# Spatial mixing of a gated MLP: the Strassen level on one chunk pair extended to both pairs, on shared combinations, with partial sums kept in PSUM

## The chip, the cores and the metric

One Trainium2 core runs the kernel; the other cores are idle. The metric is device time in microseconds, the median of 3 runs. All data are fp32 in HBM. TensorE multiplies in a reduced fp32 form, so each product of the kernel is made of three matmuls: every operand is split into a high half (written by ScalarE) and a low half (the difference, by VectorE, which the profile calls DVE), and high x high, high x low and low x high are added up in PSUM.

## The reference

```
xn = layernorm(x)                                    # 2048 x 512
# branch A: 32 heads of 16, each position attends to 8 positions, 2 apart, behind it
q, k, v = xn @ wqkv;   s = softmax(q . k[pos - 2w] / 4) . v[pos - 2w] @ wo
# branch B: gated MLP with mixing over positions
z  = gelu(xn @ w_in)                                 # 2048 x 1792
z1, z2 = z[:, :896], layernorm(z[:, 896:])
g  = w_sp @ z2 + b_sp[:, None]                       # w_sp 2048 x 2048: the spatial mixing
b  = (z1 * g) @ w_out
out = x + s * silu(b)
```

## The kernel before

The work on TensorE runs in six stages, in this order. (1) The projection to q, k and v (`product`, lines 366 to 375). (2) z1 (lines 571 to 591): seven column blocks f of 128, times four chunks c of 512 positions, transposed, stored to HBM as `z1_d` (the profile says z_d). (3) z2 (lines 593 to 666): sixteen row tiles j of 128 positions, 896 columns in two halves of 512 and 384. (4) The spatial mixing (lines 717 to 896), the stage that the change rewrites. (5) The projection with w_out (tile b, `proj` at line 905, loop at 916), sixteen row tiles of 21 matmuls. (6) The projection with wo (tile s, loop at 947), sixteen row tiles of 12 matmuls, then gate, residual and store.

**The mixing.** Its result g has seven column blocks f of 128 and four chunks c of 512 output positions. The sum runs over the sixteen z2 tiles. Chunks 2 and 3 are computed densely (line 717): for each of sixteen weight blocks and each of seven f, three matmuls of 512 columns into PSUM tile g. When a chunk is done, VectorE adds the bias for those tiles that weren't seeded with it (line 739), multiplies by z1 (line 741), and the result is parked in HBM (`g_d`); `late` fetches it again and splits it.

Chunks 0 and 1 go by one Strassen level: the weights form a 2 x 2 block matrix (chunk 0 or 1; the upper eight position tiles or the lower eight), and z2 another (upper or lower tiles; first three column blocks or last three). The middle block f = 3 is computed apart (`odd_upper`, `odd_lower`). `block_sums` (line 557) prepares the four sums of weight blocks that Strassen needs, for one position tile at a call: two loads of 512 KB, four VectorE additions of 512 columns, two stores of 512 KB to `sums_d`. `combine` (line 635) makes the four combinations T of z2 blocks in place and stores them to `t_d`; `operand` (line 749) loads two position tiles of one T and splits them into the space of the last three z2 blocks, where the original is no longer needed. `block_product` (line 760) runs one of the seven products, in four steps of two position tiles: 72 matmuls, or 96 where the middle block goes along; after each step it calls what `steps` lists. In the order p1, p2, q6, q7, q5, q3, q4 the products use the plain weights or the sums; PSUM results are copied to SBUF by ScalarE (lines 844, 882) and joined by VectorE subtractions (`minus`, line 804).

**z2 statistics.** `z2_stats` (line 614) has VectorE do two BATCH_NORM_STATS of 448 columns and one aggregation for each of sixteen tiles, then GpSimd makes the scale and shift. `z2_normal` has ScalarE normalise 896 columns in place (line 627) and then splits them.

**Attention** (line 478) is VectorE work almost alone: eight passes `sub`, each over four heads and all positions, in four steps j0 of four position tiles. A step multiplies (line 503), reduces (506), after the softmax multiplies again (530), adds in a tree (536 to 538), transposes (545) and stores to `o_d`. All of it has the lowest priority (`LOW`, lines 476 and 480).

**What sets the order.** Engines work in the order in which instructions stand on their queues. Some instructions are pinned in program order (`pin`); the rest is ordered when the kernel is compiled, by a list scheduler that simulates the time line and, among the instructions that are ready, takes the highest priority. Attention is thus placed where VectorE has nothing else that is ready.

**Buffers.** PSUM has eight banks, taken in turn by `mm`. Weights go through four raw buffers (`RAW`) and eight split pairs. Eight tiles of 1024 columns (`WIDE`, `t4`) serve z1, z2, sums, T operands and the last stage. `load_o` (line 675) fetches attention output for one group of four row tiles, one 128-row operand k of four at a time, each from two `sub` passes; k = 3 has the last one. The last stage takes the groups in the order 0, 2, 3, 1 (line 942), that is steps j0 = 0, 8, 12, 4 of each pass.

## Time and profile before

| | |
|---|---|
| median of 3 runs | 708.52 us (708.4 to 708.57) |
| profiled execution: time | 708.39 us |
| profiled execution: span, first to last instruction | 706.6 us |
| granted TensorE clock, mean | 0.999 |
| busy: TensorE / VectorE / ScalarE / GpSimd | 700.7 / 619.2 / 260.9 / 41.8 us |
| HBM read / written | 100.40 / 50.94 MB |

The stages on TensorE, from the time line of PE:

| stage | from | to |
|---|---|---|
| z2 | 227 (about 219 with its first tiles) | 294.8 |
| spatial mixing, dense chunks 2 and 3 | 294.8 | 447.2 |
| spatial mixing, chunks 0 and 1 by Strassen | 447.2 | 583.0 |
| projection with w_out | 583.0 | 659.15 |
| projection with wo | 659.15 | 703 |

A duration in a row of PE is that of one matmul from start to end, about 390 ns at 512 columns; they overlap, and their pace is the distance of two starts. A VectorE row of 0.69 us can likewise be followed after 0.60. A row of the time line gives start, duration, engine, line, operation, output <- inputs, shapes, and in brackets the idle time before it with what ended it. A row of the windows view gives the window, its length, then busy time and instruction count of PE, PEld, DVE, ACT and POOL, the granted clock, the busy share of the DMA engines and GB/s.

### The profile page before, as it was taken

To read this page: it belongs to the slowest core of one execution; us is meant where nothing else is said; L and a number is where in the kernel's file an instruction comes from. 1 tells how busy PE (TensorE), PEld (TensorE's weight loads), DVE (VectorE), ACT (ScalarE), POOL (GpSimd) and SP (SyncE) were. 2 spreads that over 40 slices of the span, in tenths; PEclk is the share of its full clock that TensorE was granted. 3 is DMA by queue.
4 is the path that set the end of the run, shared out by engine and by line. 5 is a ranking of instruction groups with operands and counts; after the bars stand their busy time and mean duration, and the time that the engine had idled before them with its cause. 6 is when DMAs were issued, how large, how long until landed. Compare 5 with 4: busy or idle time off the path is not lost.

```text
span 706.6 us, 8920 instructions
## 1 busy us (share of the span) xinstructions
PE 700.7 (99%) x3152; PEld 585.4 (83%) x3152; DVE 619.2 (88%) x770; ACT 260.9 (37%) x403; POOL 41.8 (6%) x81
## 2 busy tenths in 40 slices
PE   8999999999999999999999999999999999999997
PEld 7888888888888988888888888888888888888886
DVE  6774599989998899989999999999999999799665
ACT  4343332343224466751112211354545542131531
POOL 3100000000000443320000000000000000000000
PEclk9999999999999999999999999999999999999999
DMA  8767775585785131579956742877857781353996
GB/s 271 255 189 228 240 242 178 161 287 207 258 275 220 33 135 69 190 255 323 328 183 219 288 135 60 307 239 260 276 200 269 246 260 59 125 165 101 303 327 235
DMA packets 96652, 151.93 MB, mean 215 GB/s; under 512 B 8672, under 2 KB 50912, under 8 KB 96608
## 3 DMA queue, kind: packets, MB, share of 16 engines
q1 hardware_dynamic: 57968, 108.77, 47.1%
q10 hardware_dynamic: 38640, 42.60, 17.3%
q8 instruction: 24, 0.39, 0.2%
q14 instruction: 20, 0.16, 0.1%
HBM read 100.40 MB, written 50.94 MB: 214 GB/s over the span
## 4 chain that ended last, share of the span: by engine, by line
PE 98%; DMA 1%; DVE 0%; SPq 0%; issue 0%
PE g L695 22%; PE q L695 12%; PE p L695 6%; PE qkv L371 6%; PE qkv L373 6%; PE qkv L372 6%; PE z L608 4%; PE z L607 4%; PE z L606 4%; PE z L580 4%; PE b L911 4%; PE z L578 4%; PE b L910 4%; PE b L912 4%; PE z L579 4%; PE s L911 2%
## 5 line engine op out<-in xcount | busy, mean ns | idle before, releaser
L503 DVE TENSOR_TENSOR pr<-k,q 128x2048 f32<-128x2048 f32 x32 | 73.2, 2286 | 1.9 <-DMA q<-qkv_d 1.5
L530 DVE TENSOR_TENSOR pv<-v,lg 128x2048 f32<-128x2048 f32 x32 | 73.3, 2291 | 0.9
L506 DVE TENSOR_REDUCE lg<-pr 128x128 f32<-128x2048 f32 x32 | 73.0, 2281 | 0.4
L391 ACT ACTIVATE stage<-qkv 128x512 f32<-128x512 f32 x36 | 21.4, 596 | 49.2 <-PE qkv L373 49.1
L536 DVE TENSOR_TENSOR pv<-pv 128x1024 f32<-128x1024 f32 x32 | 39.1, 1221 | 0.5
L608 PE MATMUL z<-w_0h,BIG 128*128 128x512 f32 x64 | 25.0, 391 | 0.0
L607 PE MATMUL z<-w_0l,BIG 128*128 128x512 f32 x64 | 25.0, 391 | 0.0
L606 PE MATMUL z<-w_0h,BIG 128*128 128x512 f32 x64 | 24.9, 389 | 0.0
L921 ACT ACTIVATE bt<-b 128x512 f32<-128x512 f32 x16 | 9.4, 597 | 41.5 <-PE b L912 41.5
L627 ACT ACTIVATE zt<-zt,nmz,mvz 128x896 f32<-128x896 f32 x16 | 17.9, 1134 | 17.6 <-POOL nmz L623 17.3
L267 DVE TENSOR_TENSOR xT<-xT,mr 128x512 f32<-128x512 f32 x20 | 13.8, 688 | 11.2 <-DMA mr<-mv_d 6.6
L537 DVE TENSOR_TENSOR pv<-pv 128x512 f32<-128x512 f32 x32 | 22.0, 687 | 0.6
L608 PE MATMUL z<-w_1h,BIG 128*128 128x384 f32 x64 | 21.5, 336 | 0.0
L606 PE MATMUL z<-w_1h,BIG 128*128 128x384 f32 x64 | 21.5, 335 | 0.0
L607 PE MATMUL z<-w_1l,BIG 128*128 128x384 f32 x64 | 21.4, 335 | 0.0
L587 ACT ACTIVATE z1t<-z 128x512 f32<-128x512 f32 x21 | 12.5, 594 | 21.8 <-PE z L580 21.8
L965 DVE TENSOR_TENSOR sg<-s,sg 128x512 f32<-128x512 f32 (+1 forms) x17 | 11.2, 657 | 10.6 <-PE s L912 9.7
L618 DVE BATCH_NORM_STATS2 zst<-zt 128x6 f32<-128x448 f32 x32 | 19.1, 610 | 1.5 <-ACT zt L609 1.5
L620 POOL TENSOR_TENSOR nmz<-mvz,mone 128x1 f32<-128x1 f32 x16 | 5.0, 315 | 234.8 <-DVE mvz L619 234.7
L184 DVE TENSOR_TENSOR BIG<-zt,BIG 128x896 fp32r<-128x896 f32 x16 | 17.1, 1079 | 1.1 <-ACT BIG L183 1.1
L609 ACT ACTIVATE zt<-z 128x512 f32<-128x512 f32 (+1 forms) x24 | 12.8, 535 | 13.4 <-PE z L608 12.1
L373 PE MATMUL qkv<-wqkv_0h,BIG 128*128 128x512 f32 x43 | 16.7, 389 | 0.0
(543 smaller groups left out, 2164.1 us busy)
## 6 DMA issues: line engine op xcount, KB each, us to landing
qkv_d<-stage ACTq DMA_DIRECT2D x24, 512.0 KB
k<-qkv_d SPq DMA_DIRECT2D x8, 960.0 KB
v<-qkv_d SPq DMA_DIRECT2D x8, 960.0 KB
z_d<-z1t ACTq DMA_DIRECT2D x14, 512.0 KB
t_d<-zt ACTq DMA_DIRECT2D x16, 384.0 KB
zl<-z_d SPq DMA_DIRECT2D x12, 512.0 KB
tr<-t_d SPq DMA_DIRECT2D x16, 384.0 KB
x<-in_x SPq DMA_DIRECT2D x16, 256.0 KB
```

The costliest lines, as they stand in the source:

```text
L371: nc.tensor.matmul(pq, xh[:, k], wh, start=k == 0, stop=False)
L372: nc.tensor.matmul(pq, xh[:, k], wl, start=False, stop=False)
L373: nc.tensor.matmul(pq, xl[:, k], wh, start=False, stop=k == KB - 1)
L503: nc.vector.tensor_tensor(pr, taps(kw, j0), qb.unsqueeze(1).to_broadcast([P, W, NJ * CS]), op=ALU.mult)
L506: nc.vector.tensor_reduce(lg[:, :, j0 * HS : (j0 + NJ) * HS], pr.rearrange("p w (i d) -> p w i d", d=DH), axis=AX.X, op=ALU.add,)
L530: nc.vector.tensor_tensor(pr.rearrange("p w (i d) -> p w i d", d=DH), taps(vw, j0).rearrange("p w (i d) -> p w i d", d=DH), lg[:, :, j0 * ...
L536: nc.vector.tensor_tensor(pr[:, 0:4], pr[:, 0:4], pr[:, 4:8], op=ALU.add)
L606: nc.tensor.matmul(pz, xh[:, k], wh, start=k == 0, stop=False)
L607: nc.tensor.matmul(pz, xh[:, k], wl, start=False, stop=False)
L608: nc.tensor.matmul(pz, xl[:, k], wh, start=False, stop=k == KB - 1)
L695: nc.tensor.matmul(pg, z[a], w[b], start=start and i == 0, stop=stop and i == 2, skip_group_check=seeded)
L911: nc.tensor.matmul(pp[:, cols], hi, wl, start=False, stop=False)
```

## The change

Chunks 2 and 3 are no longer dense. Both chunk pairs go by the same Strassen level, and each of the seven products is run for the pair (2, 3) and right behind it for the pair (0, 1), so that a T operand is loaded once for two products. The order is p1, p2, q6, q5, q3, q7, q4, each for c = 2 and then for c = 0. Pair 2 has PSUM banks 4 to 7, pair 0 has 0 to 3. The signs of the combinations are chosen so that p1 + p2 + ... can go on adding in the same PSUM banks: after p1 ScalarE copies the banks to SBUF (`snapshot`), p2 adds on, after p2 the first three column blocks are gated from PSUM, the banks are seeded with the copy (`seeded`), q6 adds on, is copied, q5 adds on, is copied, and q3 adds on; q7 and q4 start from the bias. The bias is always a seed. The parked `g_d` goes; the copies after q6 are parked in `y_d` and loaded again for q4's results.

`block_sums` makes the sums of both pairs, sixteen calls for eight: seven in the z1 stage (`SUMS_Z1`), three in z2 (`SUMS_Z2`, in raw buffers), six in the steps of p1 and p2. `z2_stats` leaves VectorE: the Gelu's accumulator gives the sum, a ScalarE Square over 896 columns the variance, and GpSimd has five small operations for four. `z2_normal` splits only the first four column blocks of the upper tiles. In the last two upper and lower tiles the 384-column PSUM tile is filled with zeros by VectorE first and accumulated on. The place of the gated tiles in SBUF (`slots`) and the rows of `b_sp` are rearranged.

The diff, cut to its core:

```diff
-    def block_sums(i):
-        top, low = t4(f"sa_{i}"), t4(f"sb_{i}")
...
+    def block_sums(n, own=False):
+        c, i = 2 - n // HT * 2, n % HT
...
-        if f % 2:
-            block_sums(f // 2)
+        if f in SUMS_Z1:
+            block_sums(next(summed))
...
+        keep = h == 1 and j % HT > HT - 3
+        if keep:
+            nc.vector.memset(pz, 0.0)
...
-        nc.scalar.activation(zt[:, HALF[h]], pz, AF.Gelu_apprx_tanh, scale=late_rstd(j))
+        nc.scalar.activation(
+            zt[:, HALF[h]], pz, AF.Gelu_apprx_tanh, scale=late_rstd(j), accum_out=sumz[:, j, h : h + 1]
+        )
...
-        for h in range(2):
-            nc.vector.bn_stats(st[:, h], zt[:, h * FQ : (h + 1) * FQ])
-        nc.vector.bn_aggr(mv, st)
-        nc.gpsimd.tensor_tensor(nm, mv[:, 0:1], mone, op=ALU.mult)
-        nc.gpsimd.tensor_scalar(mv[:, 1:2], mv[:, 1:2], EPS, None, op0=ALU.add)
+        nc.gpsimd.tensor_tensor(mv[:, 0:1], sz[:, 0:1], sz[:, 1:2], op=ALU.add)
+        nc.gpsimd.tensor_scalar(mv[:, 0:1], mv[:, 0:1], -1.0 / FH, None, op0=ALU.mult)
+        nc.scalar.activation(
+            z2_at(j)[0], blocks(zt, FB), AF.Square, bias=mv[:, 0:1], accum_out=mv[:, 1:2]
+        )
+        nc.gpsimd.tensor_scalar(
+            mv[:, 1:2], mv[:, 1:2], 1.0 / FH, EPS, op0=ALU.mult, op1=ALU.add
+        )
...
-        split(zh, zl, blocks(zt, FB))
+        n = FB if j >= HT else ODD + 1
+        split(zh[:, :n], zl[:, :n], blocks(zt, FB)[:, :n])
...
-    for c in (2, 3):
-        for n, js in enumerate(order):
...
-                three(banks[key], z2_block(js, f), w, n == 0 and key not in seeds, n == NT - 1, key in seeds)
...
+    for c, b in ((2, bb[:, 1]), (0, bb[:, 0])):
+        seeded(c, "p", [b] * 3)
+        odd_[c] = seed(BANKS[c] + 3, f"oa_{c}", b)
+        if c == 2:
+            product_("p1", 2, upper, first_weights, odd_upper, ([], [sums_step], [], [sums_step]))
+    first = three_halves("s")
+    snapshot((*first[2], o1[2]), (*acc[2], odd_[2]))
+    product_("p1", 0, upper, w_sp[0, :HT], odd_upper, ([], [sums_step], [], [sums_step]))
+    snapshot((*first[0], o1[0]), (*acc[0], odd_[0]))
+    product_("p2", 2, lower, w_sp[2, HT:], odd_lower, ([T2[0]], [T2[1], sums_step], [T2[2]], [T2[3], sums_step]))
...
+    product_("p2", 0, lower, w_sp[0, HT:], odd_lower, ([g[0]], [g[1]], [], []))
+    seeded(2, "y", first[2])
+    g = first_result(0)
+    product_("q6", 2, turned, ws(2, 2), steps=([g[0]], [g[1]], [later(seeded, 0, "y", first[0])], []))
...
+    product_(
+        "q6", 0, turned, ws(0, 2),
+        steps=([later(snapshot, yv[2], acc[2]), later(store_y, 0)], [T1[0]], [T1[1]], [T1[2]]),
+    )
...
+    product_("q5", 0, turned, ws(0, 1), steps=([later(snapshot, ev[2], acc[2])], [], [], []))
...
+    product_(
+        "q3", 2, lower_right, ws(2, 4),
+        steps=([T3[0], later(snapshot, ev[0], acc[0])], [T3[1]], [T3[2]], [T3[3]]),
+    )
...
+    product_(
+        "q4", 2, turned, w_sp[3, HT:], odd_lower, steps=([T4[3], g[0]], [g[1]], [load_y], [])
+    )
...
```

More of the change, by code (lines that the diff above doesn't have):

```diff
@@ L46 @@
 WARM = 8
+SUMS_Z1 = range(7)
+SUMS_Z2 = (1, 2, 3)
 RAW = 4
@@ L658 @@
                 if i == HT - 1 and h == 0:
-                    spatial[2, HT] = spatial_block(2, HT)
+                    for js in range(2):
+                        spatial[2, js] = spatial_block(2, js)
+        if i in SUMS_Z2:
+            block_sums(next(summed), own=True)
         if 0 < i <= HT:
@@ L826, in lower_first @@
-    def lower_first(f0):
-        zl = z1_pair(1, f0, 2)
-        for f in (f0, f0 + 1):
-            v = vv[f] if f < ODD else o1
-            if f < ODD:
-                minus(v, v, banks["q", f])
-            else:
-                minus(v, banks["o", 1], v)
-            gated(1, f, v, zl[:, f - f0])
-    T1, T2, T3, T4 = [[later(operand, i, h, s0) for s0 in range(0, HT, 2)] for i, h in ((0, 0), (1, 1), (1, 0), (0, 1))]
-    block_product("p1", "p", upper, lambda s: w_sp[0, s], (0, odd_upper), start=False)
```

334 lines of the change are left out of this document (169 added, 165 removed), and 4 rows, old and new, of the table slots.

## The prediction

> **What bounds the kernel now.** I read the page's engine totals first, then its forty slices, then the chain of work that ended last.
>
> ```profile
> span 706.6 us, 8920 instructions
> PE 700.7 (99%) x3152; PEld 585.4 (83%) x3152; DVE 619.2 (88%) x770; ACT 260.9 (37%) x403; POOL 41.8 (6%) x81
> PE   8999999999999999999999999999999999999997
> DVE  6774599989998899989999999999999999799665
> ...
> 294.80 152.36 PE g L695 x672
> 447.16 43.52 PE p L695 x192
> ```
>
> TensorE is busy in every slice, and the chain runs through it for 98% of the span. The last two rows give its pace: 152.36/672 and 43.52/192 are both 0.2267 us per 512-column matmul, with no pause in 196 us. So a matmul less is 0.2267 us less, as long as nothing else comes late. The second row to read is DVE: from the sixth slice to the thirty-fourth it is nearly as full as TensorE. The windows view gives the stretch from just before the first attention work (80.4) to the last (658.65), then the z2 stage:
>
> ```profile
> 80.40:658.65 578.25, 578.25 (x2595) 484.29 (x2594) 545.42 (x626) 215.27 (x332) 31.70 (x64) 1.00 0.62 207
> 227.00:295.00 68.00, 68.00 (x339) 61.12 (x338) 65.32 (x94) 39.43 (x57) 25.09 (x51) 1.00 0.25 86
> ```
>
> DVE (third busy number) works 545.42 of 578.25 us. Attention is emitted at the lowest priority, so it fills whatever time the other DVE work leaves, and its end tells how much DVE time there was. The DVE, SP and PE timelines show how close that end is to the output projection (tile s), which needs it:
>
> ```profile
> 640.23 0.45 DVE L545 STREAM_TRANSPOSE tt<-pv 128x256 f32<-128x256 f32 x1
> 648.31 0.69 DVE L184 TENSOR_TENSOR BIG<-ol,BIG 128x512 fp32r<-128x512 f32 x1
> 651.36 0.45 DVE L545 STREAM_TRANSPOSE tt<-pv 128x256 f32<-128x256 f32 x1
> 658.20 0.45 DVE L545 STREAM_TRANSPOSE tt<-pv 128x256 f32<-128x256 f32 x1
> 663.22 0.69 DVE L184 TENSOR_TENSOR o_3l<-ol,o_3h 128x512 fp32r<-128x512 f32 x1 [0.45 <-ACT o_3h L183]
> 676.95 0.69 DVE L184 TENSOR_TENSOR o_3l<-ol,o_3h 128x512 fp32r<-128x512 f32 x1 [3.23 <-ACT o_3h L183]
> ...
> 659.15 0.39 PE L910 MATMUL s<-BIG 128*128 128x512 f32 x1
> 702.71 0.28 PE L912 MATMUL s<-BIG,o_3l 128*128 128x256 f32 x1
> ```
>
> The projection runs in four row groups of 48 matmuls, 10.9 us each. The fourth operand of a group (k=3) holds the last attention block (sub 7) and is first used 9 matmuls, 2.0 us, into it. Group one needs it at 659.15+2.0 = 661.2 and has it at 649.0: 12.2 us to spare. Group two needs it at 672.1, has it at 663.9: 8.2 us. Group three needs it at 682.9, has it at 677.6: 5.3 us. That is all the slack, and it is less than what the change takes off TensorE. So two engines bound this kernel.
>
> **TensorE's part.** Before, the spatial mixing is 2 dense chunks x 16 blocks x 7 columns x 3 = 672 matmuls, and seven products of 96 or 72 = 600; 1272. After, it is 600 for each of two pairs; 1200. 72 x 0.2267 = 16.3 us. No other matmul is added or removed. By this alone the span is 690.3 and the time, with the 1.8 us that the profiled run has outside its span (708.39 against 706.6; the median of the runs, 708.52, is 0.13 higher), 692.1. The projection would start at 642.8.
>
> **DVE's part, counted instruction by instruction.** The groups by line:
>
> ```profile
> L618 DVE BATCH_NORM_STATS2 zst<-zt 128x6 f32<-128x448 f32 x32 | 19.1, 610 | 1.5 <-ACT zt L609 1.5
> L619 DVE BATCH_NORM_AGGREGATE mvz<-zst 128x2 f32<-128x12 f32 x16 | 2.9, 194 | 0.0
> L184 DVE TENSOR_TENSOR BIG<-zt,BIG 128x896 fp32r<-128x896 f32 x16 | 17.1, 1079 | 1.1 <-ACT BIG L183 1.1
> L739 DVE TENSOR_TENSOR gt<-g,bb 128x512 f32<-128x512 f32 x8 | 5.4, 682 | 0.0
> L804 DVE TENSOR_TENSOR ya<-q,ya 128x512 f32<-128x512 f32 x4 | 2.7, 686 | 0.0
> L567 DVE TENSOR_TENSOR sb<-sa,sb 128x512 f32<-128x512 f32 x16 | 10.9, 684 | 1.8 <-issue 1.4 <-DMA sb<-in_w_sp 0.5
> L184 DVE TENSOR_TENSOR q_7l<-q_7r,q_7h 128x512 fp32r<-128x512 f32 x5 | 3.4, 686 | 0.0
> L378 DVE MEMSET mask<- 128x128 f32 x1 | 0.2, 165 | 0.0
> ```
>
> Removed: the z2 statistics, 19.1 + 2.9 = 22.0; half of eight z2 splits (512 columns instead of 896), 8 x (1.079 - 0.684) = 3.2; the eight bias additions, 5.4; two subtractions (14 remain of 16), 1.4. Together 32.0. Added: the weight sums of the second pair, 32 x 0.684 = 21.9; 24 more low-half splits of weights (112 blocks for 32 + 56), 24 x 0.686 = 16.5; a bias addition of 1024 columns for one of 512, about 0.5; four zero fills of 384 columns, 0.165 for 128 columns, so 0.2 to 0.7 each, taken 0.4, 1.6 in all. Together 40.5. The gates, the splits of the gated tiles, the T operands and the four combinations keep their number. Net +8.5 us on DVE. Some instructions start 0.60 after the one before instead of 0.69, on both sides of the account alike, so I keep 8.5, with 7 to 10 as bounds.
>
> **What that does to the end.** The last attention block ends 8.5 later, at 667, if DVE's idle time of 32.8 us stays. Group one's k=3 is then ready at 649.0 + 8.5 = 657.5, and TensorE, there at 642.8 + 2.0 = 644.9 (rounded), waits 12.6 us. The time is 692.1 + 12.6 = 704.7; the same from the other side, 708.4 + 8.5 - 12.2. For groups two and three the same step with their own slack gives 708.4 + 8.5 - 8.2 = 708.7 and 708.4 + 8.5 - 5.3 = 711.6. I take group one's. Its k=3 followed its attention block by 8.3 us (640.7 to 649.0), the others' by 12 and 19, and the SP queue shows why the last did:
>
> ```profile
> 662.02 1.90 SPq L548 DMA_DIRECT2D o_d<-tt  x4
> 669.66 0.53 SPq L971 DMA_DIRECT2D out<-sg  x1
> 671.34 3.13 SPq L678 DMA_DIRECT2D ol<-o_d  x3
> ```
>
> Group three's loads stand behind an output store that waits for the projection itself, so they move with the projection, not with attention. With 8.3 us, group two (block ended 651.8) has its operand at 651.8 + 8.5 + 8.3 = 668.6, where a projection shifted to 655.4 asks for it at 668.3: no further wait to speak of. If the idle of 32.8 shrinks by 5, 699.7.
>
> **What is hidden.** ScalarE takes over the z2 variance:
>
> ```profile
> L627 ACT ACTIVATE zt<-zt,nmz,mvz 128x896 f32<-128x896 f32 x16 | 17.9, 1134 | 17.6 <-POOL nmz L623 17.3 <-DVE mvz L619 0.3
> L183 ACT ACTIVATE wsp_13h<-wsp_13r 128x512 fp32r<-128x512 f32 x2 | 1.2, 618 | 0.0
> L844 ACT ACTIVATE ya<-p 128x512 f32<-128x512 f32 x2 | 1.2, 600 | 1.4 <-PE p L695 1.4
> ```
>
> Sixteen squarings by the 1.134 row are 18.1 us; in the z2 stage ScalarE goes from 39.4 to about 57 of 68 us. In program order, the normalisation stands behind the squaring and the next Gelu behind that, but two steps' PSUM tiles (four of eight banks each) lie between them and TensorE: nothing on the path. Later ScalarE gets 24 high halves x 0.618 = 14.8, some 13 more snapshots and 8 more seeds x 0.600 = 12.6. Each seed or snapshot falls while TensorE works on the other pair's product, 72 x 0.2267 = 16.3 us; the cover is a whole product, and if it is gone a product pays 3 x 0.6 = 1.8 us. The first products need only the upper z2 tiles, the last of them 72 matmuls after the stage begins. DMA carries more as well:
>
> ```profile
> DMA packets 96652, 151.93 MB, mean 215 GB/s; under 512 B 8672, under 2 KB 50912, under 8 KB 96608
> 660.00:680.00 20.00, 20.00 (x89) 16.54 (x89) 11.03 (x15) 6.35 (x8) 0.00 (x0) 1.00 1.02 316
> ```
>
> The second pair's sums (8.4 MB read, 8.4 written, 8.4 read back) and 6 MB more direct weights replace 8.4 MB of dense weights and 7 of parked gates, and y is parked for 3: about 19 MB on 151.93, so 171 MB in some 695 us, 246 GB/s. The fullest window moved 316 (its last two numbers: the share of the engines, GB/s), so on average the fetches, four tiles ahead, hide it.
>
> **The rivals.** *TensorE alone decides* (692 to 697). For it: the chain is 98% PE, and DVE still has 32.8 us of idle; if the new, denser mix fills about 12 of it, attention ends by 655 and nothing waits. Against it: much of the idle stands in front of splits that wait for ScalarE's halves, and ScalarE gets more of them. *The late groups decide* (711.6, slower). The place is group three's k=3, with 5.3 us of slack; the price is 8.5, so 3.2 us over the time before. It decides if the way from block to operand stays at 19 us. For it: DMA around there is full, a share of 1.02 in the window from 660 to 680. Against it: these transfers are the projection's own. *A pause slows TensorE afterwards* (706 to 708.6). A pause of 12 us on TensorE occurs nowhere here, but the opening shows a cold start:
>
> ```profile
> 1.35 3.78 PE L276 MATMUL warm<-ident 128*128 128x128 f32 x16 [1.35 <-POOL ident masks.py:199]
> 6.16 0.61 PE L276 MATMUL warm<-ident 128*128 128x128 f32 x4
> ```
>
> The same matmul takes 3.78/16 = 0.236 us first and 0.61/4 = 0.153 later, so a restart costs about 16 x 0.083 = 1.3 us, and up to three groups can restart: 704.7 + 1.3 to 3.9. The Trainium skill (TensorE: Matmul & The Clock Gate, Part 1) says that after an idle window of about 3.4 us the array runs at half clock until it has been busy for such a window; by that rule a pause of 12 us costs an estimated 1.7 us more, 706.4. The opening rows agree with the direction, though the granted clock reads 1.00 there; a pause in mid-kernel no row shows. *New waits inside the products* (705 to over 712): a zero fill waits for its PSUM bank and holds what DVE has behind it; a sum's two stores wait on ScalarE's queue for four additions, 4 x 0.684 = 2.7 us, with weight halves, snapshots and seeds behind them. For it: these queues are in order and the chain has no pause now. Against it: 16.3 us of the other pair's product lie over each. If all fourteen products paid the 1.8 us, it would be 25 us, so the place matters more than the price.
>
> **How the numbers follow.** Forecast, attention's end with group one's slack, 698 to 708.7: 0.40. TensorE alone: 0.20. Late groups: 0.22. Cold restarts on top: 0.10. Waits inside the products: 0.08. A measurement here can tell about 0.2%, so "same" is 707.0 to 709.8. Faster: nearly all of the forecast's chance (0.36), 0.20, a third of the cold case (0.03), 0.02; 0.61. Same: 0.04 + 0.05 + 0.03 from these and 0.01 from the products; 0.13. Slower: the rest, 0.26. The range runs from TensorE's floor, 692.0, to the late groups', 711.6; the forecast's own is 698 to 708.7.
>
> **What would show it.** Line 695's successor has 1200 matmuls at 0.2267. DVE is busy about 627 us. The last transpose of attention ends near 667, and the first pause of TensorE over 2 us stands in the projection, released by an o operand, around 645 to 657. If TensorE has no pause there, the forecast is wrong on the fast side; if attention ends at 667 and the pauses are in groups two and three, it is the late groups; if TensorE pauses before the projection, the step that failed is that the products' waits are hidden.

## The result and the profile after

The changed kernel takes 720.22 us (median of 4 runs, 718.18 to 720.89) against 708.46 us before (4 runs, 708.14 to 708.57): a ratio of 1.0162, interval 1.0141 to 1.0183. The forecast was 704.7 with a range of 692.0 to 711.6, so it is wrong, on the other side. The profiled execution took 718.18 us, 716.4 of it span, which is 9.8 us more than the span before. Of the runs reported below, one of e4 (1835 us) and one of e12 (3979 us) were disturbed and are left out; both were the profiled ones, so that e4 was run again, and of e12's profile only the order of the instructions is used.

The page of the changed kernel: totals, TensorE's slices and clock, and the chain by engine.

```profile
span 716.4 us, 9058 instructions
PE 689.0 (96%) x3080; PEld 573.3 (80%) x3080; DVE 624.7 (87%) x771; ACT 300.3 (42%) x512; POOL 51.1 (7%) x97
PE   8999999999999999599999999999999999999973
PEclk9999999999999999899999999999999999999997
...
PE 81%; DMA 6%; DVE 4%; ACT 3%; issue 2%; SPq 1%; POOL 1%; ACTq 1%; DVEq 0%
```

The counts are near the predicted ones: 72 matmuls fewer, DVE at 624.7 us (627 predicted), 170.8 MB of DMA (171 predicted). What is new is the 5 in TensorE's seventeenth slice, at 286.6 to 304.5 us, with a dip in the clock under it, and two lean slices at the end. TensorE's share of the chain fell from 98% to 81%. TensorE's waits over the whole span, with total, number and longest:

```profile
PE p L734 <- ACT wsp_0h L188: 6.6, 1, 6.6
PE s L966 <- ACT o_3h L188: 3.6, 1, 3.6
PE s L966 <- DVE sg L1021: 1.4, 1, 1.4
...
PE z L633 <- ACT zt L637: 1.1, 1, 1.1
```

The TensorE and DVE timelines give the stage borders and the last attention transpose:

```profile
302.94 1.65 PE L734 MATMUL p<-wsp_0h,BIG 128*128 128x512 f32 x3 [6.61 <-ACT wsp_0h L188]
...
681.56 0.45 DVE L550 STREAM_TRANSPOSE tt<-pv 128x256 f32<-128x256 f32 x1
...
653.35 0.39 PE L966 MATMUL s<-BIG 128*128 128x512 f32 x1
...
704.12 0.28 PE L968 MATMUL s<-BIG,o_3l 128*128 128x256 f32 x1
```

The mixing begins at 302.94 (before: 294.63), the next stage at 577.19 (582.99), the projection at 653.35 (659.15), and the last matmul ends at 704.40 (702.99). So the 9.8 us are:

| part | us |
|---|---|
| 72 matmuls fewer | -16.3 |
| z2 stage ends later and TensorE pauses before the products | +8.3 |
| within the products (half clock after the pause, a gap of 0.4) | +2.2 |
| projection: 51.05 us instead of 43.84 (pauses of 3.6 and 1.4, slow matmuls after the first) | +7.2 |
| from the last matmul to the end: 12.0 us instead of 3.6 | +8.4 |

There are two places of loss: the z2 stage at 300 us, 10.5 us, and the projection with its tail, 15.6 us.

**The first place.** Around the pause the windows show TensorE idle (0.39 busy of 7) and VectorE and ScalarE full; the clock (third number from the end) then takes 3 us to come back:

```profile
80.40:682.00 601.60, 592.13 (x2645) 494.16 (x2643) 560.58 (x639) 260.00 (x449) 41.42 (x80) 0.99 0.70 236
296.00:303.00 7.00, 0.39 (x3) 0.07 (x2) 6.88 (x8) 6.97 (x16) 2.46 (x8) 0.71 0.36 123
303.00:306.00 3.00, 3.00 (x8) 2.21 (x9) 3.00 (x6) 3.00 (x7) 2.10 (x3) 0.53 0.71 248
306.00:310.00 4.00, 4.00 (x19) 3.29 (x18) 4.00 (x5) 4.00 (x10) 1.80 (x4) 1.00 1.01 400
```

ScalarE's timeline says what it does while TensorE waits for the first weight half (wsp_0h):

```profile
263.44 1.05 ACT L648 ACTIVATE BIG<-zt,mvz 128x896 fp32r<-128x896 f32 x1 [1.75 <-POOL mvz L647]
264.39 0.19 ACT L648 ACTIVATION_READ_ACCUMULATOR BIG<-zt,mvz 128x1 f32 x1
...
266.69 1.14 ACT L659 ACTIVATE zt<-zt,nmz,mvz 128x896 f32<-128x896 f32 x1 [1.66 <-POOL nmz L655]
...
302.27 0.62 ACT L188 ACTIVATE wsp_0h<-wsp_0r 128x512 fp32r<-128x512 f32 x1
...
307.98 0.48 ACT L637 ACTIVATE zt<-z 128x384 f32<-128x384 f32 x1
```

The Squaring (L648) waits 1.75 us for a mean that GpSimd forms, the normalisation (L659) 1.66 us for GpSimd's next steps. Every instruction with a sum beside its output is followed by a second one of 0.19 us. TensorE's last z2 matmul started at 296.00, and its Gelu runs at 307.98: ScalarE is 12 us behind, and the weight half sits in its queue. The change had also moved that half: the kernel before split the first weight block ahead of z2, at 201.7 (`early_pair`), and the changed kernel asks for it only near the end of z2. The four seeds of the first product were written by 299.7, so by an estimate about 3.2 of the 6.6 us (302.9 - 299.7) would go if the early split had stayed; no run restores it. It matters only when ScalarE is late: e1 and e17 below do without it and have no pause. Over 219 to 330 us ScalarE's waits add up to:

```profile
ACT zt L659 <- POOL nmz L655: 11.0, 7, 2.2
ACT BIG L648 <- POOL mvz L647: 10.7, 6, 2.9
```

**The second place.** The last attention block ends at 682.0; before it was 658.65. In the window from 80.4 to its end, VectorE works 560.58 of 601.60 us and idles 41.0 (before: 545.42, idle 32.8). So the end moved by 23.4 us = 15.2 more work in the window + 8.2 more idle. Only 5.5 of the 15.2 is work that the change added (624.7 - 619.2 over the whole kernel). The other 9.7 is VectorE work of later stages, which was done behind attention's end before and is now ahead of it. When the last block is there, SyncE's queue brings what is left late:

```profile
692.16 0.36 SPq L1027 DMA_DIRECT2D out<-sg  x1
692.63 1.28 SPq L717 DMA_DIRECT2D ol<-o_d  x1
...
696.68 0.33 SPq L988 DMA_DIRECT2D sg<-b_d  x1
```

The last operand load and the four pairs of loads for the last outputs (696.68 to 700.11) stand behind output stores, and are issued when TensorE is nearly through. In the chain that ended last, the load issued at 699.61 takes 8.7 us to land, at 708.4, and the last gates follow it. That is the tail.

### The profile page after: what moved, and what is told of

The parts are those of the page before. It is cut to its first block, busy times and chain, and to the rows that moved or that the text cites. A ratio compares the mean times of both kernels' runs of the same rounds, so it can differ in the third digit from the quotient of the medians.

```text
span 716.4 us, 9058 instructions
## 1 busy us (share of the span) xinstructions
PE 689.0 (96%) x3080; PEld 573.3 (80%) x3080; DVE 624.7 (87%) x771; ACT 300.3 (42%) x512; POOL 51.1 (7%) x97
## 4 chain that ended last, share of the span: by engine, by line
PE 81%; DMA 6%; DVE 4%; ACT 3%; issue 2%; SPq 1%; POOL 1%; ACTq 1%; DVEq 0%
PE y L734 14%; PE q L734 9%; PE p L734 8%; PE z L633 7%; PE qkv L378 4%; PE qkv L377 4%; PE qkv L376 4%; PE z L601 4%; PE b L968 4%; PE b L967 4%; PE z L600 4%; PE z L602 4%; PE b L966 4%; PE ob L734 3%; PE oa L734 3%
## 5 line engine op out<-in xcount | busy, mean ns | idle before, releaser
L508 DVE TENSOR_TENSOR pr<-k,q 128x2048 f32<-128x2048 f32 x32 | 73.1, 2285 | 2.7 <-DMA q<-qkv_d 2.4
L511 DVE TENSOR_REDUCE lg<-pr 128x128 f32<-128x2048 f32 x32 | 73.0, 2280 | 0.4
L633 PE MATMUL z<-w_0h,BIG 128*128 128x512 f32 x128 | 41.3, 392 | 1.1 <-ACT zt L637 1.1
L541 DVE TENSOR_TENSOR pv<-pv 128x1024 f32<-128x1024 f32 x32 | 39.0, 1218 | 0.3
L633 PE MATMUL z<-w_1h,BIG 128*128 128x384 f32 x128 | 34.0, 336 | 0.0
L633 PEld LDWEIGHTS z<-w_0h,BIG 128*128 128x128 f32 x128 | 24.0, 188 | 6.6 <-ACT zt L637 1.8
L582 DVE TENSOR_TENSOR sa<-sa,sa 128x512 f32<-128x512 f32 x39 | 26.5, 681 | 2.0 <-DMA sa<-in_w_sp 1.6
L646 POOL TENSOR_TENSOR mvz<-sumz 128x1 f32<-128x1 f32 x16 | 9.7, 605 | 204.7 <-ACT zt L637 204.7
L633 PEld LDWEIGHTS z<-w_1h,BIG 128*128 128x128 f32 x128 | 23.3, 188 | 0.3
L609 ACT ACTIVATE z1t<-z 128x512 f32<-128x512 f32 x21 | 12.4, 592 | 25.0 <-PE z L602 18.5
L659 ACT ACTIVATE zt<-zt,nmz,mvz 128x896 f32<-128x896 f32 x16 | 18.1, 1134 | 11.2 <-POOL nmz L655 11.0
L189 DVE TENSOR_TENSOR BIG<-zt,BIG 128x512 fp32r<-128x512 f32 (+1 forms) x16 | 14.2, 888 | 9.3 <-ACT BIG L188 9.1
L648 ACT ACTIVATE BIG<-zt,mvz 128x896 fp32r<-128x896 f32 x16 | 16.6, 1039 | 12.4 <-POOL mvz L647 10.7
L188 ACT ACTIVATE BIG<-zl 128x512 fp32r<-128x512 f32 x28 | 17.3, 621 | 10.0 <-DVE zl L807 8.5
L188 ACT ACTIVATE BIG<-tr 128x768 fp32r<-128x768 f32 x16 | 13.4, 843 | 17.8 <-PE q L734 9.1
```

What stands on the lines that cost most here:

```text
L188: first_ = pin(nc.scalar.activation(hi, src, AF.Copy))
L508: nc.vector.tensor_tensor(pr, taps(kw, j0), qb.unsqueeze(1).to_broadcast([P, W, NJ * CS]), op=ALU.mult)
L511: nc.vector.tensor_reduce(lg[:, :, j0 * HS : (j0 + NJ) * HS], pr.rearrange("p w (i d) -> p w i d", d=DH), axis=AX.X, op=ALU.add,)
L541: nc.vector.tensor_tensor(pr[:, 0:4], pr[:, 0:4], pr[:, 4:8], op=ALU.add)
L633: nc.tensor.matmul(pz, a[:, k], b, start=k + i == 0 and not keep, stop=k == KB - 1 and i == 2, skip_group_check=keep,)
```

## The experiments

Two theories stood at the start. A: VectorE's amount of work, through attention's end, sets the time. B: the pause after z2 does. Each kernel was timed beside the kernel before on the same chip, whose median was 708.2 to 708.5. Ratios are to that.

**Statistics back on VectorE (e1).** The changed kernel, with the z2 statistics as before (lines joined and cut):

```
-        nc.scalar.activation(z2_at(j)[0], ..., AF.Square, bias=mv[:, 0:1], accum_out=mv[:, 1:2])
+            nc.vector.bn_stats(st[:, h], zt[:, h * FQ : (h + 1) * FQ])
+        nc.vector.bn_aggr(mv, st)
```

> The changed kernel with the z2 statistics on VectorE again, as before the change; all else stays. Theory A (attention's end on VectorE sets the end, and the pause in front of the products only moves TensorE's idle time): the pause of 6.6 us goes, VectorE gets 22.0 us more work and loses some 12 us of idle time in the z2 stage, so attention ends near 692 instead of 682 and the time is about 730. Theory B (the z2 stage, now bound by ScalarE, is the main loss): z2 ends at 294.8 and the products follow without a pause, and the time is about 710.

Measured: 725.61 us (724.41 to 729.04), ratio 1.0252 [1.0223, 1.0280]. The mixing begins at 294.7, so the pause after z2 is gone. But VectorE is busy 642.4 us, the last transpose comes at 692.5, and the products and the projection wait:

```profile
PE y L734 <- DVE pv L544: 9.6, 1, 9.6
PE s L966 <- ACT o_3h L190: 5.6, 1, 5.6
```

So the pause is not all: taking it away by loading VectorE costs more. A stands, B alone falls.

**The weight sums on GpSimd (e2), and both edits together (e3).**

```
-            nc.vector.tensor_tensor(parts[out_], parts[a], parts[b], op=ALU.add)
+            nc.gpsimd.tensor_tensor(parts[out_], parts[a], parts[b], op=ALU.add)
```

> The changed kernel with all 64 additions of the weight sums on GpSimd instead of VectorE. VectorE loses 64 x 0.684 = 43.8 us of work, GpSimd gets about 64 x 1.3 = 83 us. Theory A: attention ends near 639, no wait is left in the last projection and its tail is 3.6 us as before; the pause in the z2 stage stays, so 692.1 + 10.5 = 702.6. Theory B: the same place loses less, since the z2 stage sets the end: 715 or more. Rival: GpSimd's additions delay the small GpSimd steps of the z2 statistics or VectorE itself, and nothing is won: 720 or more.

> Both edits at once: z2 statistics on VectorE, weight sums on GpSimd. VectorE's work is 21.8 us less than in the changed kernel and its waits for ScalarE in the z2 stage go, so attention ends near 649 and TensorE does not wait anywhere: 692 to 696. If a limit other than VectorE's work and the z2 stage holds the changed kernel back (DMA, or the order of the last loads), it stays above 702.

Measured: e2 737.30 (737.08 to 737.84), 1.0410 [1.0393, 1.0427]; e3 732.99 (730.20 to 733.48), 1.0340 [1.0320, 1.0360]. VectorE lost 64 additions of 0.684 us, 43.8 us, and yet its busy time rose from 624.7 to 636.8. The groups of e2, attention's operations and the additions (busy, mean ns):

```profile
L508 DVE TENSOR_TENSOR pr<-k,q 128x2048 f32<-128x2048 f32 x32 | 78.0, 2438 | 1.6 <-DMA q<-qkv_d 1.2
...
L511 DVE TENSOR_REDUCE lg<-pr 128x128 f32<-128x2048 f32 x32 | 73.0, 2280 | 0.3
L541 DVE TENSOR_TENSOR pv<-pv 128x1024 f32<-128x1024 f32 x32 | 45.4, 1418 | 0.4
L542 DVE TENSOR_TENSOR pv<-pv 128x512 f32<-128x512 f32 x32 | 27.1, 847 | 0.6
```

```profile
L582 POOL TENSOR_TENSOR sa<-sa,sa 128x512 f32<-128x512 f32 x39 | 68.0, 1745 | 190.5 <-DMA z_d<-z1t 111.1 <-DMA sa<-in_w_sp 33.5 <-ACT w_1h L188 14.4
```

In the changed kernel the same VectorE rows are 2285, 2280, 1218 and 684 ns: the two-input operations of these rows got 7 to 24% slower, the one-input reduction not at all. Splits that fell beside GpSimd's additions suffered most (the three of p_7l took 1768 ns in the mean, 682 in the changed kernel). The Trainium skill (SBUF — State Buffer, Who interferes with whom) says that a VectorE instruction with two SBUF inputs contends with a GpSimd instruction that reads SBUF, and that a reduction does not. The rows agree. GpSimd cannot take all of this work here; a part of it was not tried.

**Half of attention left out (e5).** The changed kernel, with four of the eight attention passes computed and stored twice:

```
-    for sub in range(NSUB):
+    for sub in range(0, NSUB, 2):
```

> The changed kernel with four attention passes of eight computed; each result is stored for two passes, so the attention output of every second pass is that of its neighbour. VectorE loses about 190 us of work. What is left is what the mixing costs without attention's end behind it: under both theories the pause in the z2 stage stays and the last projection has no wait, 702 to 704. If it comes to 692, the pause was itself attention's doing; if it stays above 710, the late end is not attention's.

Measured: 714.14 us (711.51 to 717.36), 1.0081 [1.0055, 1.0107]. By its number this is above 710, the expectation's case that the late end is not attention's; the trace says otherwise. VectorE is busy 466.6 us, the projection takes 43.8 us without a wait and 4.4 us follow it: the second loss is attention's. The time stays high because the first loss stays and is larger: the mixing begins at 310.7 instead of 302.9.

```profile
310.73 1.65 PE L735 MATMUL p<-wsp_0h,BIG 128*128 128x512 f32 x3 [9.56 <-ACT wsp_0h L188]
```

So the two losses have different causes, and the pause is not VectorE's amount of work.

**The statistics alone (e4), in the kernel before.** Only z2_stats is exchanged, and the two Gelus give their sums.

> The kernel before with only the z2 statistics moved to ScalarE, as the change does it; mixing, sums and order stay as before. VectorE has 22.0 us less. Theory C (the z2 stage itself is bound by ScalarE and the way over GpSimd, whatever follows): a pause of some 8 to 10 us between z2 and the mixing, 716 to 719, with attention ending earlier. Rival (the pause comes only from the changed kernel's seeds, sums and weight splits in that stage): no pause, 708.4.

> The kernel before with the z2 statistics on ScalarE once more, for its profile; the first time gave 724.0, some 16 us over the kernel before. Theory C: TensorE pauses 10 to 16 us in z2 and between z2 and the mixing, waiting for ScalarE, and nowhere else, while attention ends 15 us or more ahead of 658.65. Rival: the loss sits at the end, behind attention, and the z2 stage has no pause.

Measured: 724.03 and, run again, 723.84 us (723.28 to 724.40), 1.0216 [1.0195, 1.0236]. No Strassen level is added, VectorE has 18 us less to do (601.3), attention ends at 653.6, five us early, and the kernel is 15.5 us slower. TensorE's waits, and the window of the z2 stage:

```profile
PE g L698 <- ACT zt L610: 8.7, 3, 3.7
...
PE g L698 <- ACT wsp_8h L184: 0.5, 1, 0.5
```

```profile
219.00:315.00 96.00, 86.73 (x403) 74.78 (x402) 76.55 (x84) 66.26 (x129) 40.76 (x72) 0.92 0.37 124
```

Pauses of 9.2 us, and 8% of 86.7 us lost to the clock (0.92 in this window), an estimated 6.9: together 16. This kernel has the early split of the first weight block, so its loss does not come from there. A part that the prediction put at nothing costs as much as the 72 matmuls bring.

**Work or waits? (e14, e15, in the kernel before.)** e14 adds ScalarE's work and none of its waits; e15 has the waits and most of the work taken out (the variance is of 8 columns only; its lines are shown against e4).

```
e14 +        nc.scalar.activation(z2_at(j)[0], blocks(zt, FB), AF.Square, accum_out=sumz[:, j, 0:1])
e15 -            z2_at(j)[0], blocks(zt, FB), AF.Square, bias=mv[:, 0:1], ...
e15 +            z2_at(j)[0][:, 0, :8], blocks(zt, FB)[:, 0, :8], AF.Square, bias=mv[:, 0:1], ...
```

> The kernel before with ScalarE's extra work but without its extra waits: the two Gelus of a z2 tile also give their sums, and a Square of the tile is done and its sum thrown away; the statistics stay on VectorE, so nothing waits for the Square but the split behind it on the same engine. W (the work alone makes ScalarE late): 16 x (1.04 + 3 x 0.19) = 26 us more on ScalarE in a stage of 68 to 76 us, TensorE pauses before the mixing as with the statistics moved, 718 to 730. R (the round trips to GpSimd make it late): 708 to 711, and the mixing begins near 294.7.

> The kernel before with the z2 statistics on ScalarE and GpSimd as in the change, but the Square takes 8 of the 896 columns, so the variance leaves out the others: the same waits, with about 0.8 us less work per tile, 13 us in all. W: 708 to 713. R: 718 to 724, as with the whole Square (723.8). Something between on both would say that the two add up.

Measured: e14 708.57 us (708.00 to 709.22), 1.0003 [0.9993, 1.0012]; e15 716.39 us (716.22 to 716.62), 1.0113 [1.0098, 1.0128]. The first rows are ScalarE's stretch of z2, from its first Gelu to its last split, in e14, e15 and e4 (its busy time is the fourth). The second are its waits for GpSimd there, in the same order:

```profile
220.90:313.90 93.00, 93.00 (x455) 82.49 (x454) 88.72 (x128) 70.18 (x138) 33.04 (x64) 1.00 0.34 117
...
219.90:315.50 95.60, 89.85 (x429) 79.03 (x428) 81.52 (x91) 61.66 (x137) 45.67 (x80) 0.96 0.40 133
...
220.30:325.20 104.90, 95.63 (x437) 81.95 (x436) 84.28 (x94) 73.70 (x140) 46.44 (x80) 0.92 0.37 122
```

```profile
ACT zt L631 <- POOL nmz L627: 16.7, 9, 4.5
...
ACT zt L630 <- POOL nmz L626: 14.6, 13, 2.3
ACT BIG L619 <- POOL mvz L618: 12.9, 10, 3.3
...
ACT zt L630 <- POOL nmz L626: 16.6, 10, 3.1
ACT BIG L619 <- POOL mvz L618: 11.1, 8, 3.3
```

From 219 to 295, 13.6 us more work on ScalarE (55.66 in e14 against 42.05 before) cost nothing. The waits with 7 us more work (49.02 in the same window) cost 8.1 us, and with all the work (e4) 15.5. Work and waits stand in one queue, so they add. Over the windows shown the sum is 70.2 + 16.7 = 86.9 us in e14, 61.7 + 27.5 = 89.2 in e15 and 73.7 + 27.7 = 101.4 in e4; in the same way it is 70.7 in the kernel before and 74.0 + 21.7 = 95.7 in the changed kernel. TensorE does not pause at 70.7 and 86.9, and pauses more the higher the sum: 5.7 us at 89.2 (e15), 7.7 at 95.7 (the changed kernel), 9.2 at 101.4 (e4).

**One wait taken away (e13).** The changed kernel with a Square of the unshifted values, which needs no mean; GpSimd gets two more steps (square of the mean, subtraction).

> The changed kernel with the Square taken of the unshifted values, so that it waits for no mean: the variance is the mean square less the squared mean, with two more small GpSimd steps. ScalarE's work stays the same. If the pause in front of the products comes from ScalarE waiting on GpSimd between Gelu and Square, it falls below 3 us and VectorE's idle time in z2 with it: 708 to 714. If it is ScalarE's work in that stage, the pause stays at 5 us or more: 716 to 721.

Measured: 727.85 us (727.46 to 729.47), 1.0281 [1.0267, 1.0295], worse than the change. The pause before the products is 7.6 us, and 4.8 us of pauses come within z2; ScalarE's sum is 73.9 + 28.3 = 102.2. The wait moved to the next instruction in the queue:

```profile
ACT zt L659 <- POOL nmz L655: 28.3, 11, 4.2
```

**The waits put under other work (e16, e17).** e16 keeps the changed kernel's statistics and their work, but forms a tile's mean in the step of its Gelus, squares a step later and normalises two steps later, each between Gelus of other tiles and held in that order. e17 does this and has SyncE issue the stores of T and of the sums formed in z2.

```
e16 +                if h == 0 and i > 1:
    +                    z2_normal(a * HT + i - 2, raw_z[i - 2][a])
    +                if h == 1 and 0 < i <= HT:
    +                    z2_square(a * HT + i - 1, raw_z[i - 1][a])
    +                if i < HT:
    +                    z2_half(a * HT + i, h, raw_z[i][a])
...
e17 -            nc.scalar.dma_start(t_d[a, i], src)
    +            nc.sync.dma_start(t_d[a, i], src)
```

> The changed kernel with the same statistics on ScalarE and GpSimd, the same work, in another order: the mean of a tile is formed in the step of its Gelus, its Square runs a step later and its normalisation two steps later, each between Gelus of other tiles and kept in that order, so that GpSimd's steps lie under other work of ScalarE. R (the round trips make ScalarE late): the pause of 6.6 us before the products and the 1.5 within z2 go, with the half-clocked matmuls behind them, and VectorE's idle time in z2 with them, so attention ends near 671 to 676 instead of 682: 703 to 712. W (the amount of work): no change, 718 to 722. If attention's end alone sets the time and does not move, 718 as well, but with the mixing starting near 295.

> The kernel of e16_round_trips_apart with the 16 stores of T and the 12 stores of the sums formed in z2 issued by SyncE instead of ScalarE. There ScalarE still waited 33 us from 219 to 330, but 29 of it in front of instructions that stood behind stores waiting for VectorE's combinations and additions, and 9 for GpSimd. Q (ScalarE's in-order queue is late through whatever it waits for in z2, statistics or stores): with both kinds of waits gone the pauses in z2 and before the products go, the mixing starts near 295 to 297, and attention's end falls below the 682 of the changed kernel: 703 to 714. W (the amount of work): pauses of 5 us or more stay, 718 or more. If SyncE is held up instead, weights or attention operands come late and TensorE waits for a weight's high half inside the products.

Measured: e16 745.65 us (744.38 to 745.92), 1.0523 [1.0506, 1.0541]; e17 711.08 us (708.96 to 713.65, 8 runs), 1.0038 [1.0025, 1.0052]. In e16 ScalarE waits little for the means (1.2 us), but behind stores on its own queue that wait for VectorE (from 219 to 330 us):

```profile
ACT BIG L652 <- DVE sr L582: 12.5, 1, 12.5
...
ACT BIG L652 <- DVE pv L543: 7.1, 1, 7.1
```

With these stores on SyncE, e17's first product starts behind the last z2 matmul without a pause. Its timeline, the window to attention's end and TensorE's longest wait (this profiled run is the slowest of the eight, 713.65, span 711.9):

```profile
294.18 0.33 PE L633 MATMUL z<-w_1h,BIG 128*128 128x384 f32 x1
294.36 0.63 PE L749 MATMUL p<-wsp_0h,BIG 128*128 128x512 f32 x2
```

```profile
80.40:676.65 596.25, 591.86 (x2644) 492.60 (x2642) 559.94 (x639) 261.21 (x449) 50.96 (x80) 1.00 0.70 238
```

```profile
PE s L981 <- ACT o_3h L188: 3.2, 1, 3.2
```

The z2 loss is gone with the same work on ScalarE, and 9.1 of the change's 11.8 us with it. ScalarE's z2 work and its waits for GpSimd are 78.8 + 8.1 = 86.9 us, as in e14. e17 differs from the changed kernel in two things, the order and the queue of the stores; the stores alone on SyncE were not run, but in the changed kernel ScalarE waits 1.7 us for a store ahead of the products and 21.7 for GpSimd. Of the versions that leave nothing out it is the fastest with both Strassen levels, and still 0.4% slower than the kernel before: the products have short waits, 3.0 us in those listed, and the projection waits as in the change, because attention ends at 676.65.

**VectorE's slack (e6, e7), in the kernel before.** Additional maxima of a block with itself, which change no value: 12 of them, and 32.

```
+        for n in range(1 + i % 2):
+            nc.vector.tensor_tensor(top[:, n], top[:, n], top[:, n], op=ALU.max)
```

> The kernel before with 12 VectorE instructions that change nothing, 12 x 0.686 = 8.2 us, about the net work that was counted for the change. With 32 of them (21.9 us) it was 16.3 us slower, which leaves a slack of 5.6 us. Forecast's step (group one's slack of 12.2 decides): no change, 708.4. Slack of 5.3 to 5.6 (group three): 8.2 - 5.5 = 2.7 us slower, 711. Attention's end moves by more than the work added, as with 32: up to 714.

> The kernel before with 32 more VectorE instructions of 512 columns that change nothing (the maximum of a tile with itself) behind the weight sums: 32 x 0.684 = 21.9 us more VectorE work, the mixing unchanged. Theory A in numbers: in the changed kernel and in the one with the statistics on VectorE the span ends 34.4 us after attention (682.0 to 716.4, 692.9 to 727.2); attention would end near 680.6 here, so span 715 and time 717. If attention's end is not what decides, 708 to 710.

Measured: e6 708.55 us (708.22 to 710.29, 11 runs), 1.0009 [1.0000, 1.0018]; e7 724.69 (722.83 to 726.18), 1.0229 [1.0211, 1.0247]. VectorE's busy time rose by 5.3 us (to 624.5) and by 15.5 (to 634.7). The last transposes, e6 first:

```profile
670.71 0.43 DVE L545 STREAM_TRANSPOSE tt<-pv 128x256 f32<-128x256 f32 x1
```

```profile
686.51 0.45 DVE L545 STREAM_TRANSPOSE tt<-pv 128x256 f32<-128x256 f32 x1
```

Attention's end moves 12.5 us for 5.3 of added busy time, and 28.3 for 15.5. The surplus, 7 and 13 us, is not proportional to the work: most of it is VectorE work of the last stage that was done behind attention's end and is now ahead of it (26.6 us behind the end before, 20.0 in e6, 17.1 in e7). At 671.1 TensorE still has no pause; at 687.0 the kernel pays 16.4 us. e6 adds as much VectorE time as the change does (5.5) and costs 0.3 us, so that amount by itself is free in the kernel before.

**Fewer additions, and no sums (e8, e9, e11).** All three have the statistics on VectorE as e1. e8 leaves out all additions of the weight sums and stores raw blocks in their place, e9 leaves out half, e11 forms, stores and loads no sums and multiplies with raw blocks.

```
e8  -            nc.vector.tensor_tensor(parts[out_], parts[a], parts[b], op=ALU.add)
e11 -        return sums_d[c // 2, half_, :, :, a]
    +        return w_sp[c + a, half_ * HT : (half_ + 1) * HT]
```

> The changed kernel with the statistics on VectorE and without the 64 additions of the weight sums: the raw blocks are stored in the sums' place, so the products use wrong weights; loads, stores and everything else stay. Theory A: attention ends near 692.9 - 43.8 = 649, TensorE waits nowhere: 692 to 695, the gain that the matmul count promised. If DMA, the order of the last loads or the seeds are a bound of their own, it stays above 700.

> As the run without additions, but with those of every second weight block: 32 additions, 21.9 us more VectorE work than without. Theory A, with attention's end 34.4 us ahead of the span's: attention ends near 671, span 705.4, time 707. If VectorE's work has a threshold instead of a slope, 692 to 696 or 720.

> As the run without additions, but the sums' loads and stores are gone too: products that use a sum read a raw block of the weights instead, so they use wrong weights. 16.8 MB less read and 16.8 MB less written. The run without additions came to 703.5 with 8 us of waits inside the products. Theory D (the DMA traffic around the first products, a share of 0.9 to 1.0 of the engines, makes weights late): the waits go, 692 to 695. If they come from the order of the queues, it stays at 700 or more.

Measured: e8 703.47 us (702.28 to 704.00), 0.9929 [0.9914, 0.9943]; e9 709.31 (707.51 to 710.34), 1.0011 [1.0002, 1.0021]; e11 694.32 (694.04 to 694.60), 0.9798 [0.9782, 0.9814]. e11 matters most: with sums at no cost the span is 692.8 and no wait of TensorE is left from z2 on, as the slices of e11 show. In e8, with the sums' transfers and no additions, it waits 7.8 us within the products, nearly all for halves of weights; 4.5 of that fall in a stretch where the DMA share is 0.92 (second number from the end; in e11 it is 0.70):

```profile
PE   8999999999999999999999999999999999999996
```

```profile
295.00:380.00 85.00, 80.40 (x347) 64.23 (x346) 73.85 (x90) 36.37 (x59) 8.26 (x10) 1.00 0.92 323
```

The sums' loads and stores cost 9.2 us (703.47 - 694.32), the first half of the additions another 5.8, the second half 16.3 (725.61 - 709.31). In VectorE's busy time the halves are 17.5 and 18.5 us (606.4, 623.9, 642.4): the slack is used up on the way, and the second half costs 0.9 us for each.

**A mixture (e10), and earlier loads (e12).** e10 has the statistics of half the tiles on ScalarE and of the others on VectorE; e12 is e10 with the last groups' loads a group earlier.

```
e10 +        if j % HT > 3:
    +            return dve_stats(j, zt)
e12 -            fetched[i + 4] = fetch_pair(i + 4, arrived[groups[min(i // NJ + 1, 3)]])
    +            fetched[i + 4] = fetch_pair(i + 4, arrived[groups[min(i // NJ, 3)]])
```

> The changed kernel with the statistics of tiles 0 to 3 and 8 to 11 on ScalarE and of the other eight on VectorE. The pause in front of the products goes or falls below 3 us, since ScalarE has nothing of the kind left at the end of z2. VectorE gets 11 us of work and loses most of its 15 us of idle time in z2. Theory A: attention ends at 678 to 687 and the span 34.4 later, time 714 to 723. If the pause was the larger part of the loss, 708 to 710.

> The run with mixed statistics, and the last stage's gate and residual loads wait for the attention operands of the group at hand instead of the next one. In the changed kernel four pairs of these loads stood behind the last group's operands (696.7 to 700.1) and the span ended 12.0 us after the last matmul instead of 3.6. If that is a loss of its own, it comes out 4 to 8 us under the run with mixed statistics; if these loads are bound by DMA, the same.

Measured: e10 720.98 us (719.86 to 721.87), 1.0175 [1.0160, 1.0190], with 4.1 us of pauses before the products, 8.4 within them, and attention's end at 688.3. e12 723.93 (721.20 to 725.02), 1.0204 [1.0179, 1.0230]. The order of the last loads, as far as e12 changes it, brings nothing; in its queue two of the four pairs of loads still stand behind the last operand load.

## Why the prediction was wrong

**TensorE's part held.** The product lines have 72 matmuls fewer, and e11 shows the saving: its output projection starts at 643.0, where 642.8 was worked out, and its span is 692.8, where it was 690.3.

**VectorE's count was near, and too high.** +5.5 us measured, +8.5 predicted with bounds of 7 to 10; busy 624.7 for 627. One reading beside it was wrong without bearing on the result: the window of 316 GB/s was not the fullest by rate, since the page before has a slice at 328.

**What is hidden: this step failed first.** The prediction put the squaring in "the z2 stage ScalarE goes from 39.4 to about 57 of 68 us" and "nothing on the path". The prediction's own test, a pause ahead of the projection, points to this part. The count had the work and left out the waits, although the row quoted beside it has them: 17.6 us in front of the normalisations. The squaring brought a second trip to GpSimd per tile, and a second short instruction for each of three sums per tile. Work plus waits for GpSimd over z2 becomes 95.7 us, against 70.7 before. The cover that the prediction named, PSUM tiles of two steps, did hold inside z2 (a pause of 1.1 us). What came late was the first weight half, which stands in the same queue and which the change itself had moved to the end of z2. Shown: the statistics alone cost the kernel before 15.5 us (e4), the work alone 0.3 (e14), the waits with little work 8.1 (e15); with the waits put under other work, and the stores on SyncE, the pause goes and the time falls from 720.22 to 711.08 (e17). What is late in z2 also holds VectorE: its idle time from 219 us to the products is 15.0 us in the change (2.8 before).

**What that does to the end: this step failed too.** "The last attention block ends 8.5 later, at 667, if DVE's idle time of 32.8 us stays." It ended 23.4 later. The terms are 5.5 of added work (8.5 predicted), 8.2 of idle time, which is the failed step above, and 9.7 of other stages' VectorE work that now lies ahead of attention's end, which the prediction left out. Attention has the lowest priority. When its end slides into the projection, the projection's own evictions and additions go ahead of it, and each moves it further. e17, with the first cause gone, has 18.0 = 5.2 + 9.3 + 3.5 by the same windows. The windows behind attention's end, before and after the change, show that passing over (VectorE's is the third busy number):

```profile
658.65:706.60 47.95, 44.34 (x207) 37.00 (x206) 26.62 (x36) 13.48 (x18) 0.00 (x0) 0.99 0.88 292
...
682.00:716.40 34.40, 18.68 (x84) 15.26 (x84) 17.00 (x25) 8.14 (x9) 0.00 (x0) 0.84 0.78 287
```

It is a term of limited size and not a factor: 17 us stay behind the end in e1, e7, e9 and e17 as well, and between e9 and e1, where nothing more passes over, attention's end moves 16.7 us for 18.5 us of busy time.

The place of the wait was wrong as well. The prediction had TensorE wait for group one's k=3, 2.0 us into the projection. That operand came 15.7 us later than before (664.7 for 649.0), and TensorE did not wait for it: in the changed kernel's compiled order it is used from 666.73, 13.4 us into the projection, behind first operands of the next group. The 3.6 us are for an o_3h of a later group (684.28), loaded after the last attention block. Nor does e6 test the 12.2 us of slack that were worked out for group one: its last block ends 12.5 us later without a pause, but group one's operand comes only 6.0 us later (655.0).

From attention's end to the span's end there are 34.4 us in the change, 34.3 in e1, 34.0 in e7, 35.2 in e13 and e17, 31.0 in e10 and 30.2 in e9. So in these kernels the end is attention's end plus 30 to 35 us, unless TensorE is later. By that, an estimate for an end at 667 is a span of 697 to 702, near the 702.9 of the forecast. That nearness is luck, since the wait that the forecast priced does not occur; the size of the miss is in where attention ends. What the 30 to 35 us are made of was not taken apart.

**The rivals.** TensorE alone deciding is what e11 shows, when the sums cost nothing. Late groups: the projection's pauses are in the late groups, on o_3h and then on an eviction, with the last loads behind stores in SyncE's queue; that is what happens once attention is late, though the rival's 711.6 priced neither cause. A pause slows TensorE afterwards: 3 us at a clock of 0.53 after 6.6 us of idleness, where a matmul starts every 0.42 us instead of 0.23; a loss of about 3 x 0.47 = 1.4 us, near the 1.3 that was priced, in another place. After 3.6 us of idleness the clock is 0.57 (684.28 to 687.50); after 1.4 us it is 1.00. The Trainium skill (TensorE: Matmul & The Clock Gate, Part 1) has half clock after an idle window, until about 3.4 us of work; the windows agree with it. Waits inside the products: the change has 0.4 us of them, e1 and e8 have 11 and 8.

**What stays open.** Whether the sums' transfers make weights late by their share of the DMA engines or by their places in SyncE's queue was not separated (e8 and e11 differ in both). How much of the first pause the early split of the first weight block would have saved, and what the stores on SyncE bring without the new order, was not run. Whether e17's attention could end earlier with the same work was not tried.

## What to carry to other kernels

Count an in-order engine's time in a stage as work plus the waits that its rows show, and add a wait for every trip to another engine that an edit brings; an engine at 57 of 68 us by work alone may have no room. Before an edit moves work off a full engine, try that edit by itself: here the move alone cost as much as the main change brought. Work that runs at the lowest priority ends later by more than what is put ahead of it when its end slides into the next stage, by as much of that stage's work as passes it (here up to 10 us); put that work into the sum. Where a scheduler orders the instructions, a late operand can be used later too, so a slack read from the old order may not hold in the new one.

## What the runs showed of the hardware that was not expected

- A ScalarE instruction that also gives a sum along its row is followed by an ACTIVATION_READ_ACCUMULATOR of 0.18 to 0.20 us. It overlaps with its neighbours: the one at 264.39 starts 0.10 us before its ACTIVATE ends, and the next instruction starts at 264.48. So e14's added work, expected at 26 us from the durations, came to 16.9 of busy time (277.8 against 260.9).
- GpSimd needs 1.55 to 1.91 us (means of the groups in e2) for a 128x512 addition that takes VectorE 0.684, and meanwhile slows VectorE's two-input operations, those of 512 columns from 684 to 847 ns in the mean of attention's and to 1768 for single splits.
- Five stores that stood together in ScalarE's queue and waited for VectorE, three of sums and two of T, held ScalarE for 12.5 us in e16, more than half of all its waits for GpSimd in the changed kernel in that stage (21.7); on which queue a store is issued can matter that much.
